# Sliding-window attention and maxout feed-forward on one core: Q and K of two batches loaded in groups of six tiles and transposed on the tensor engine, in a new order

## The chip, the cores and the metric

The kernel runs on one core of one Trainium2 chip. The metric is device time in microseconds (us), and lower is better. Executions of one kernel differ by a few tenths of a microsecond, so each comparison below takes several executions of both kernels on the same chip.

Engines: PE is the tensor engine, PEld its weight loads, DVE the vector engine, ACT the scalar engine, POOL is GpSimd, SP is the engine whose queue issues nearly all transfers. PE writes its results into PSUM, in units called banks; an eviction copies one from there to SBUF and frees the bank. The pitch of a kind of work is the time from one start to the next. "Landing" is the moment at which all data of a transfer have arrived.

## The reference

```python
# B, H, S, D = 4, 8, 768, 64;  n_global = 8;  n_local = 96
scores = q @ k.T / sqrt(D)                       # per batch and head
keep   = (key < n_global) | (0 <= query - key < n_local)
scores = scores + bias(head, distance)           # linear in the distance, one slope a head
a      = softmax(where(keep, scores, -1e9))
x      = (a @ v) laid out as 3072 tokens x 512
h      = maximum(maximum(x @ w1, x @ w2), x @ w3)   # d_ff = 768
return h @ w_out                                 # float32, 3072 x 512
```

## The kernel before

The 3072 tokens are 24 tiles of 128, six to a batch. A query tile needs only its own keys, those of the tile before and the eight global keys (copied into the tile before). Everything is cast to bf16. Q and K need their head dimension on the partitions, so they must be transposed; so must the attention result x before the feed-forward matmuls. Each transposition can be done in two ways: on PE (a matmul with the identity into a PSUM bank, then an eviction by ACT or DVE) or by a DMA transpose on the SP queue, which costs PE nothing.

What each engine does, and when, is a string of units. Each engine works through its own share of the string in order:

- `lG.p`, `cG.p`, `xG.p`: load, cast and transpose on PE part p of group G of tiles (Q and K);
- `LT`, `CT.0`, `XT`: load, cast and transpose Q and K of a single tile T (`XT.4` is a DMA transpose);
- `v`, `S`, `M`, `A`: load of v, scores with exp, mask multiply on DVE, attention output of a tile; a score unit whose last digit is 1 adds the bias on PE instead of having a mask multiplied later; `G` and `V` copy the global keys and values;
- `TT`: transpose x of tile T (`.4` by DMA, else on PE);
- `Fc.f.j`: first feed-forward matmuls of chunk c; `O` and `E`: second feed-forward and store; `w`, `W`, `o`, `Q`: load and cast weights; `K`, `B`: masks and biases; `D`: warm-up matmuls.

A group of sz tiles is loaded with sz consecutive tokens to a partition, so one row of a transfer is sz x 256 bytes: 512, 1024 or 1536.

```python
GROUPS = [[0, 2], [2, 2], [4, 2], [6, 4], [10, 2]]   # first tile, tiles
sizes = [4, 2, 2, 4, 4, 4, 4]                        # tiles of a feed-forward chunk
...
xb_pool  = ctx.enter_context(tc.tile_pool(name="xb", bufs=3))
ost_pool = ctx.enter_context(tc.tile_pool(name="ost", bufs=4))
psH = ... bufs=3   # tag "h":  feed-forward, and half of the transposes
psT = ... bufs=1   # tag "tp": transposes

def load_part(n, s):
    ...
    nc.sync.dma_start(out=r, in_=src.rearrange("h (i e) d -> i h (e d)", e=sz))

def u_x(n, s, how):                  # a part of a group, transposed on PE
    ...
    for e in range(sz):
        for j in range(lo, hi):
            nc.tensor.transpose(tp[:, e, j - lo], ..., identb)
    ...
    copy(dst[:, lo:hi], tp.rearrange("c e j i -> c j i e"))   # dst "c j (i e) -> c j i e"

def u_XT(T, how):                    # x of tile T
    ...
    if how == 4:
        nc.sync.dma_start_transpose(out=xT[c][:, :, i * 128:(i + 1) * 128], in_=...)
        return
    ...                              # else four PE transposes and one copy

def f2_out(po, c, tt, copy, ...):    # final eviction and store
    ost = ost_pool.tile(...)
    copy(ost, po)
    dma.dma_start(out=out[...], in_=ost)
```

The softmax here doesn't subtract the row's maximum and nothing guards it: scores larger than these inputs give would overflow.

Of the kernel before, what the change touches and what calls it, by code (L numbers as in the profile page):

```python
# [22 lines left out]


SCHEDULE = """
    K0 K1 K2 K3 K4 K5 l1.0 l1.1 D0.3 c0.0.2 B0.1 B1.1 B2.1 B3.0 K6 B4.1 B5.1 c0.1.1 c1.0.2 x0.0.4 B6.1
    B7.1 x0.1.4 S0.0.1 v0 l2.0 l2.1 K7 S0.1.1 G0.0 S1.0.1 S1.1.0 x1.0.3 c1.1.2 M0.0 M0.1 M1.0 v1 x1.1.4
    C0.1.2 v2 A0.1 G1.2 S2.0.1 M1.1 c2.0.2 x2.0.1 C1.1.1 S2.1.0 G2.2 S3.0.1 M2.0 M2.1 C2.1.1 T0.1 S3.1.1
    M3.0 M3.1 c2.1.2 v3 A1.0 C3.1.0 w0.0 V1.2 x2.1.2 w1.0 A2.1 V2.2 A3.0 T1.0 T2.1 T3.1 W1.0.1 W0.0.0
    G3.2 S4.0.0 S4.1.0 F0.0.0 F0.1.0 M4.0 F0.2.0 F0.3.0 G4.1 S5.0.0 M4.1 S5.1.0 w0.1 W0.1.1 w0.2 W0.2.2  # L30
    V3.2 F0.0.1 F0.1.1 F0.0.2 F0.1.2 v4 C4.1.0 A4.0 V4.2 w1.1 W1.1.2 W2.0.0 F0.4.0 F0.5.0 M5.0 M5.1 w1.2
    W1.2.2 v5 W2.1.0 T4.0 F0.2.1 F0.3.1 l3.0 l3.2 F0.4.1 l3.1 c3.0.2 c3.2.2 F0.5.1 o2 C5.1.0 A5.1 l3.3
    F0.2.2 Q2.2 F0.3.2 W2.2.0 o0 T5.0 F0.4.2 o1 F0.5.2 x3.0.0 F1.0.0 F1.1.0 c3.1.1 F1.2.0 x3.2.0 Q0.2
    F1.0.1 F1.1.1 F1.2.1 l4.0 l4.1 c3.3.0 F1.0.2 F1.1.2 F1.2.2 x3.1.2 x3.3.1 F1.3.0 F1.4.0 Q1.2 F1.3.1
    S6.0.0 S6.1.0 v6 v7 v8 G6.0 F1.3.2 F1.5.0 v9 c4.0.1 F1.4.1 S7.0.0 S7.1.0 G7.2 v10 M6.0 M6.1 M7.0
    M7.1 O0.0.0 F1.4.2 c4.1.1 C6.1.2 C7.1.2 L12 F1.5.1 S8.0.0 S8.1.0 x4.0.0 O0.1.0 A6.0 x4.1.2 A7.1 V7.2
    F1.5.2 v11 T6.0 O0.2.0 T7.1 G8.2 C8.1.2 S9.0.0 S9.1.0 G9.1 v12 v13 O0.3.0 F2.0.0 F2.1.0 S10.0.0 M8.0
    M8.1 M9.0 M9.1 S10.1.0 C9.1.2 L13 L14 F2.0.1 F2.1.1 F2.0.2 A8.0 C12.0.1 F2.1.2 G10.2 O1.0.0 V8.2
    A9.1 X12.1 M10.0 M10.1 C10.1.0 C11.1.0 F2.2.0 S11.0.0 S11.1.0 M11.0 M11.1 L15 F2.3.0 F2.4.0 O1.1.0
    V9.2 A10.1 F2.2.1 V10.2 T8.0 F2.3.1 F2.5.0 T9.0 A11.1 F2.4.1 T10.0 F2.2.2 F2.3.2 T11.1 F2.4.2  # L40
    S12.0.0 S12.1.0 F2.5.1 C13.0.2 C14.0.2 C15.0.1 X13.4 F3.0.0 F3.1.0 F3.0.1 G12.1 C12.1.0 F3.2.0
    F3.1.1 F3.2.1 S13.0.0 S13.1.0 F2.5.2 v14 C13.1.0 C14.1.2 M12.0 M12.1 F3.0.2 F3.1.2 X14.4 F3.2.2
    X15.4 G13.2 M13.0 M13.1 S14.0.0 S14.1.0 F3.3.0 F3.4.0 F3.5.0 M14.0 M14.1 G14.1 A12.0 A13.1 F3.3.1
    F3.4.1 F3.5.1 S15.0.0 M15.0 S15.1.0 G15.0 v15 V13.2 L16 L17 v16 T12.4 v17 M15.1 O2.0.0 C15.1.0 A14.0
    V14.2 F3.3.2 F3.4.2 T13.4 F3.5.2 C16.1.0 C16.0.2 X16.3 T14.4 C17.0.2 A15.1 X17.4 O2.1.0 S16.0.0
    S16.1.0 G16.1 L18 V15.2 L19 T15.1 M16.0 O3.0.0 M16.1 F4.0.0 F4.1.0 F4.0.1 F4.1.1 C18.0.2 L20 C19.0.2
    A16.1 F4.2.0 F4.3.0 S17.0.0 S17.1.0 F4.2.1 F4.0.2 F4.3.1 v18 M17.0 v19 M17.1 X18.3 X19.4 C20.0.0
    V16.2 F4.1.2 C17.1.2 O3.1.1 A17.1 F4.2.2 F4.3.2 S18.0.0 M18.0 S18.1.0 M18.1 F4.4.0 T16.4 T17.4
    F4.4.1 C18.1.2 C19.1.1 F4.4.2 X20.4 G18.1 S19.0.0 S19.1.0 F4.5.0 L21 M19.0 M19.1 v20 F4.5.1 A18.0
    T18.4 F4.5.2 A19.1 T19.4 V19.1 C21.0.1 X21.4 G19.1 L22 C22.0.2 L23 X22.4 O3.2.1 O3.3.0 O4.0.1  # L50
    S20.0.0 S20.1.0 M20.0 G20.0 O4.1.0 F5.0.0 F5.1.0 F5.2.0 S21.0.0 S21.1.0 G21.2 F5.0.1 F5.1.1 M20.1
    M21.0 F5.3.0 F5.0.2 F5.1.2 F5.2.1 F5.2.2 v21 C20.1.1 C21.1.2 F5.4.0 S22.0.0 M21.1 S22.1.0 C23.0.0
    F5.3.1 M22.0 M22.1 F5.5.0 F5.3.2 A20.0 V20.2 G22.2 v22 F5.4.1 X23.4 v23 F5.5.1 T20.4 A21.1 V21.1
    T21.4 F5.4.2 F5.5.2 S23.0.0 S23.1.0 M23.0 O4.2.0 M23.1 C22.1.2 A22.0 C23.1.0 O4.3.0 V22.2 T22.4
    A23.1 T23.4 O5.0.1 O5.1.0 O5.2.1 O5.3.0 F6.0.0 F6.1.0 F6.0.1 F6.0.2 F6.2.0 F6.3.0 F6.4.0 F6.1.1
    F6.2.1 F6.1.2 F6.3.1 F6.4.1 F6.2.2 F6.3.2 F6.5.0 F6.4.2 F6.5.1 F6.5.2 E
"""


# [450 lines left out]
```

## Time and profile before

The median was 180.36 us, from 180.34 to 180.45 in three runs. From the page of the profile (span 178.5 us):

| | busy us | share of the span |
|---|---|---|
| PE | 167.1 | 94% |
| DVE | 119.1 | 67% |
| ACT | 103.2 | 58% |
| POOL | 37.4 | 21% |
| main DMA queue (time of its packets over 16 engines) | | 83.6% |
| DMA packets, of them under 512 bytes | 83,587 / 66,160 | |

Read it so: one engine stands out, and it is PE. But a share of the whole span is an average over stages. The stretches that the prediction shows give the stages: until 23.3 us PE has gaps, from there to 172 us it has almost none, and then come the final stores.

I use three measures of a trace throughout: the start (until the first feed-forward matmul begins), the body (from there until the first of the final evictions begins) and the tail (from the first to the last of those evictions). Before, they end at 23.27, 172.04 and 175.46 us: the body takes 148.77 us and the tail 3.42.

### The profile page before, as it was taken

The numbers are of one execution on the slowest core, as the hardware profiler recorded it, in microseconds if no ns is written. First come the engines' busy times: TensorE is split into PE (matmuls) and PEld (weight loads), VectorE is DVE, ScalarE is ACT, GpSimd is POOL, SyncE is SP. The second block draws the span as 40 slices with busy tenths as digits, with TensorE's granted clock in tenths as the row PEclk, the third lists the DMA queues.
The fourth block names the chain that finished last, engine by engine and source line by source line (L and its number), as shares of the span: only waits on it lengthen the run. The fifth ranks groups of instructions, "written<-read, shape, count | busy, mean of one in ns | idle before, by whom it ended". The sixth has DMA issues, their size and how long they took to land.

```text
span 178.5 us, 3963 instructions
## 1 busy us (share of the span) xinstructions
PE 167.1 (94%) x1529; PEld 95.9 (54%) x1551; DVE 119.1 (67%) x237; ACT 103.2 (58%) x160; POOL 37.4 (21%) x65
## 2 busy tenths in 40 slices
...
GB/s 139 292 270 243 357 321 383 319 361 356 252 194 229 218 254 227 142 204 234 92 90 122 167 253 231 145 172 152 182 156 300 123 129 147 252 12 4 0 47 190
DMA packets 83587, 35.52 MB, mean 199 GB/s; under 512 B 66160, under 2 KB 78320, under 8 KB 83568
## 3 DMA queue, kind: packets, MB, share of 16 engines
q1 hardware_dynamic: 83424, 35.20, 83.6%
...
q10 hardware_dynamic: 144, 0.07, 0.1%
...
HBM read 25.17 MB, written 6.29 MB: 176 GB/s over the span
## 4 chain that ended last, share of the span: by engine, by line
PE 88%; ACT 3%; DVE 2%; POOL 2%; issue 1%; DMA 1%; POOLq 0%; ACTq 0%
PE h L361 53%; PE po L376 16%; PE sp L283 7%; PE op L322 3%; PE op L325 3%; PE tpp L239 3%; PE xtp L349 2%; ACT wmask L300 2%; PE sp L275 2%; DMA out_dram<-ost 1%; DVE qkT L243 1%; DVE xb L332 1%; ACT ost L382 1%; ACT P L288 1%; PE tp L261 1%
## 5 line engine op out<-in xcount | busy, mean ns | idle before, releaser
L361 PE MATMUL h<-xT,w 128*128 128x512 bf16 (+1 forms) x491 | 99.2, 348 | 0.7 <-issue 0.2
L361 PEld LDWEIGHTS <-w 128*128 128x128 bf16 x504 | 47.0, 98 | 40.4 <-ACT w L427 0.2
L288 ACT ACTIVATE P<-sp 128x1024 bf16<-128x1024 f32 (+1 forms) x48 | 43.4, 954 | 20.4 <-PE sp L283 20.2
L368 DVE TENSOR_TENSOR h<-h,h 128x512 bf16<-128x512 bf16 (+1 forms) x42 | 25.2, 609 | 25.6 <-PE h L361 15.5
L366 ACT CAST h<-h 128x512 bf16<-128x512 f32 (+1 forms) x42 | 21.6, 532 | 21.5 <-PE h L361 21.3
L376 PE MATMUL po<-wo,ht 128*128 128x512 bf16 (+2 forms) x147 | 33.1, 362 | 0.5
L370 DVE TENSOR_TENSOR ht<-h,h 128x512 bf16<-128x512 bf16 (+1 forms) x42 | 25.0, 606 | 3.7 <-PE h L361 3.0
L307 DVE TENSOR_TENSOR P<-P,wmask 128x1024 bf16<-128x1024 bf16 x36 | 24.8, 716 | 3.6 <-ACT P L288 3.5
L382 ACT COPY ost<-po 128x512 f32<-128x512 f32 (+2 forms) x20 | 11.2, 564 | 18.4 <-PE po L376 11.2
L376 PEld LDWEIGHTS <-ht 128*128 128x128 bf16 x156 | 14.0, 98 | 13.8
L332 DVE TENSOR_TENSOR xb<-op,rz 128x512 bf16<-128x512 f32 x24 | 16.6, 691 | 0.8
L283 PEld LDWEIGHTS <-qkT 64*128 64x128 bf16 x352 | 10.2, 96 | 10.0 <-issue 8.0
L283 PE MATMUL sp<-qkT 64*128 64x128 bf16 x352 | 15.2, 223 | 0.4 <-DVE xb L332 0.4
L322 PEld LDWEIGHTS <-P 128*128 128x128 bf16 x192 | 12.5, 97 | 2.7 <-ACT P L288 0.2
L221 POOL COPY va<-vaf 8x260 int32<-8x260 int32 x14 | 6.3, 449 | 34.7 <-PE op L325 34.7
L198 POOL CAST qkb<-raw 128x1024 bf16<-128x1024 f32 x7 | 7.2, 1037 | 27.6 <-DMA raw<-in_k_dram 27.6
L322 PE MATMUL op<-va,P 128*128 128x65 bf16 x160 | 12.4, 193 | 0.3 <-ACT va L189 0.2
L239 PE MATMUL tpp<-identb,qkp 128*128 128x128 bf16 x96 | 8.5, 246 | 4.0 <-POOL qkp L183 3.5
L325 PEld LDWEIGHTS <-P 128*128 128x128 bf16 x160 | 10.4, 97 | 1.8 <-issue 0.2
L239 PEld LDWEIGHTS <-qkp 128*128 128x128 bf16 x96 | 7.0, 112 | 5.8 <-POOL qkp L183 4.4
L325 PE MATMUL op<-va,P 128*128 128x65 bf16 x128 | 9.9, 193 | 0.1
L243 ACT COPY qkT<-tpp 128x1024 bf16<-128x1024 bf16 (+1 forms) x9 | 7.9, 873 | 3.4 <-PE tpp L239 3.4
...
## 6 DMA issues: line engine op xcount, KB each, us to landing
...
rawp<-in_q_dram SPq DMA_DIRECT2D x6, 512.0 KB, 7.3
rawp<-in_k_dram SPq DMA_DIRECT2D x6, 512.0 KB, 7.7
...
wst<-in_moe_w_dram SPq DMA_DIRECT2D x3, 512.0 KB, 8.6
```

The source lines that it names most:

```text
L239: nc.tensor.transpose(tp[:, e, j - lo], qb["p", n, s][:, e, 2 * j:2 * j + 2].rearrange("i h d -> i (h d)"), identb)
L283: nc.tensor.matmul(sp[:, hh, j2, ds], qT(T - ds, 1)[hsl, jp], qT(T, 0)[hsl, jp], start=not how, stop=True, skip_group_check=True)
L288: nc.scalar.activation(P[:, :, 0:n], sp.rearrange("p a b d n -> p (a b) d n")[:, :, 0:n], AF.Exp, bias=0.0, scale=scale)
L307: nc.vector.tensor_mul(P, P, wmask[:, g, :, 0:2])
L322: nc.tensor.matmul(o, P[:, i, 0], heads(va[T])[:, h], start=True, stop=(t == 0), skip_group_check=True)
L325: nc.tensor.matmul(o, P[:, i, 1], heads(va[T - 1])[:, h], start=False, stop=True, skip_group_check=True)
L332: nc.vector.tensor_tensor(out=x.rearrange("p (g h) d -> p g h d", g=2), in0=o4[:, :, :, 0:64], in1=rz[:, :, :, None].to_broadcast([128, 2, ...
L361: nc.tensor.matmul(ps, w123[f // 2][:, dm, j, (f % 2) * 128:(f % 2) * 128 + 128], xT[c][:, dm], start=(dm == 0), stop=(dm == 3))
L366: nc.scalar.copy(h01, ps)
L368: nc.vector.tensor_max(h01s[c, f], h01s[c, f], ps)
L370: nc.vector.tensor_max(ht[c][:, f], h01s[c, f], ps)
L376: nc.tensor.matmul(po, ht[c][:, f, tt * 128:(tt + 1) * 128], wo[:, f, cols], start=(f == 0), stop=(f == NF - 1))
```

## The change

The intent: Q and K of two whole batches (tiles 6 to 17) come in two groups of six tiles with rows of 1536 bytes and are transposed on PE. Before, it was one group of four and one of two in batch 1, and single tiles with rows of 256 bytes after that. This should relieve the DMA queue, which then has room for more transposes of x by DMA. The whole order was planned anew.

```diff
-    GROUPS = [[0, 2], [2, 2], [4, 2], [6, 4], [10, 2]]
+    GROUPS = [[0, 2], [2, 2], [4, 2], [6, 6], [12, 6]]

 SCHEDULE = """
-    K0 K1 K2 K3 K4 K5 l1.0 l1.1 D0.3 c0.0.2 B0.1 B1.1 B2.1 B3.0 K6 B4.1 B5.1 c0.1.1 c1.0.2 x0.0.4 B6.1
-    ... (all 31 lines of the order)
+    K0 K1 l1.0 l1.1 B0.1 B1.1 B2.2 B3.1 B4.0 B5.0 B6.1 c0.0.0 B7.1 c0.1.1 c1.0.2 x0.0.3 K2 K3 K4 x0.1.4
+    ... (all 32 lines of the order)
```

Counted from the two orders:

| | before | after |
|---|---|---|
| Q and K transposes on PE (128x128) | 120 | 144 |
| Q and K tiles transposed by DMA | 9 | 6 |
| x tiles transposed on PE / by DMA | 13 / 11 | 8 / 16 |
| score units with the bias on PE | 6 | 7 |
| warm-up units | 1 | 0 |
| tiles of Q and K loaded one by one | 12 | 6 |

More of the change, by code (lines that the diff above doesn't have):

```diff
@@ L25 @@
 SCHEDULE = """
-    K0 K1 K2 K3 K4 K5 l1.0 l1.1 D0.3 c0.0.2 B0.1 B1.1 B2.1 B3.0 K6 B4.1 B5.1 c0.1.1 c1.0.2 x0.0.4 B6.1
-    B7.1 x0.1.4 S0.0.1 v0 l2.0 l2.1 K7 S0.1.1 G0.0 S1.0.1 S1.1.0 x1.0.3 c1.1.2 M0.0 M0.1 M1.0 v1 x1.1.4
-    C0.1.2 v2 A0.1 G1.2 S2.0.1 M1.1 c2.0.2 x2.0.1 C1.1.1 S2.1.0 G2.2 S3.0.1 M2.0 M2.1 C2.1.1 T0.1 S3.1.1
-    M3.0 M3.1 c2.1.2 v3 A1.0 C3.1.0 w0.0 V1.2 x2.1.2 w1.0 A2.1 V2.2 A3.0 T1.0 T2.1 T3.1 W1.0.1 W0.0.0
-    G3.2 S4.0.0 S4.1.0 F0.0.0 F0.1.0 M4.0 F0.2.0 F0.3.0 G4.1 S5.0.0 M4.1 S5.1.0 w0.1 W0.1.1 w0.2 W0.2.2
@@ L31 @@
-    V3.2 F0.0.1 F0.1.1 F0.0.2 F0.1.2 v4 C4.1.0 A4.0 V4.2 w1.1 W1.1.2 W2.0.0 F0.4.0 F0.5.0 M5.0 M5.1 w1.2
-    W1.2.2 v5 W2.1.0 T4.0 F0.2.1 F0.3.1 l3.0 l3.2 F0.4.1 l3.1 c3.0.2 c3.2.2 F0.5.1 o2 C5.1.0 A5.1 l3.3
-    F0.2.2 Q2.2 F0.3.2 W2.2.0 o0 T5.0 F0.4.2 o1 F0.5.2 x3.0.0 F1.0.0 F1.1.0 c3.1.1 F1.2.0 x3.2.0 Q0.2
-    F1.0.1 F1.1.1 F1.2.1 l4.0 l4.1 c3.3.0 F1.0.2 F1.1.2 F1.2.2 x3.1.2 x3.3.1 F1.3.0 F1.4.0 Q1.2 F1.3.1
-    S6.0.0 S6.1.0 v6 v7 v8 G6.0 F1.3.2 F1.5.0 v9 c4.0.1 F1.4.1 S7.0.0 S7.1.0 G7.2 v10 M6.0 M6.1 M7.0
@@ L36 @@
-    M7.1 O0.0.0 F1.4.2 c4.1.1 C6.1.2 C7.1.2 L12 F1.5.1 S8.0.0 S8.1.0 x4.0.0 O0.1.0 A6.0 x4.1.2 A7.1 V7.2
-    F1.5.2 v11 T6.0 O0.2.0 T7.1 G8.2 C8.1.2 S9.0.0 S9.1.0 G9.1 v12 v13 O0.3.0 F2.0.0 F2.1.0 S10.0.0 M8.0
-    M8.1 M9.0 M9.1 S10.1.0 C9.1.2 L13 L14 F2.0.1 F2.1.1 F2.0.2 A8.0 C12.0.1 F2.1.2 G10.2 O1.0.0 V8.2
-    A9.1 X12.1 M10.0 M10.1 C10.1.0 C11.1.0 F2.2.0 S11.0.0 S11.1.0 M11.0 M11.1 L15 F2.3.0 F2.4.0 O1.1.0
-    V9.2 A10.1 F2.2.1 V10.2 T8.0 F2.3.1 F2.5.0 T9.0 A11.1 F2.4.1 T10.0 F2.2.2 F2.3.2 T11.1 F2.4.2
@@ L41 @@
-    S12.0.0 S12.1.0 F2.5.1 C13.0.2 C14.0.2 C15.0.1 X13.4 F3.0.0 F3.1.0 F3.0.1 G12.1 C12.1.0 F3.2.0
-    F3.1.1 F3.2.1 S13.0.0 S13.1.0 F2.5.2 v14 C13.1.0 C14.1.2 M12.0 M12.1 F3.0.2 F3.1.2 X14.4 F3.2.2
-    X15.4 G13.2 M13.0 M13.1 S14.0.0 S14.1.0 F3.3.0 F3.4.0 F3.5.0 M14.0 M14.1 G14.1 A12.0 A13.1 F3.3.1
-    F3.4.1 F3.5.1 S15.0.0 M15.0 S15.1.0 G15.0 v15 V13.2 L16 L17 v16 T12.4 v17 M15.1 O2.0.0 C15.1.0 A14.0
-    V14.2 F3.3.2 F3.4.2 T13.4 F3.5.2 C16.1.0 C16.0.2 X16.3 T14.4 C17.0.2 A15.1 X17.4 O2.1.0 S16.0.0
@@ L46 @@
-    S16.1.0 G16.1 L18 V15.2 L19 T15.1 M16.0 O3.0.0 M16.1 F4.0.0 F4.1.0 F4.0.1 F4.1.1 C18.0.2 L20 C19.0.2
-    A16.1 F4.2.0 F4.3.0 S17.0.0 S17.1.0 F4.2.1 F4.0.2 F4.3.1 v18 M17.0 v19 M17.1 X18.3 X19.4 C20.0.0
-    V16.2 F4.1.2 C17.1.2 O3.1.1 A17.1 F4.2.2 F4.3.2 S18.0.0 M18.0 S18.1.0 M18.1 F4.4.0 T16.4 T17.4
-    F4.4.1 C18.1.2 C19.1.1 F4.4.2 X20.4 G18.1 S19.0.0 S19.1.0 F4.5.0 L21 M19.0 M19.1 v20 F4.5.1 A18.0
-    T18.4 F4.5.2 A19.1 T19.4 V19.1 C21.0.1 X21.4 G19.1 L22 C22.0.2 L23 X22.4 O3.2.1 O3.3.0 O4.0.1
@@ L51 @@
-    S20.0.0 S20.1.0 M20.0 G20.0 O4.1.0 F5.0.0 F5.1.0 F5.2.0 S21.0.0 S21.1.0 G21.2 F5.0.1 F5.1.1 M20.1
-    M21.0 F5.3.0 F5.0.2 F5.1.2 F5.2.1 F5.2.2 v21 C20.1.1 C21.1.2 F5.4.0 S22.0.0 M21.1 S22.1.0 C23.0.0
-    F5.3.1 M22.0 M22.1 F5.5.0 F5.3.2 A20.0 V20.2 G22.2 v22 F5.4.1 X23.4 v23 F5.5.1 T20.4 A21.1 V21.1
-    T21.4 F5.4.2 F5.5.2 S23.0.0 S23.1.0 M23.0 O4.2.0 M23.1 C22.1.2 A22.0 C23.1.0 O4.3.0 V22.2 T22.4
-    A23.1 T23.4 O5.0.1 O5.1.0 O5.2.1 O5.3.0 F6.0.0 F6.1.0 F6.0.1 F6.0.2 F6.2.0 F6.3.0 F6.4.0 F6.1.1
@@ L56 @@
-    F6.2.1 F6.1.2 F6.3.1 F6.4.1 F6.2.2 F6.3.2 F6.5.0 F6.4.2 F6.5.1 F6.5.2 E
+    K0 K1 l1.0 l1.1 B0.1 B1.1 B2.2 B3.1 B4.0 B5.0 B6.1 c0.0.0 B7.1 c0.1.1 c1.0.2 x0.0.3 K2 K3 K4 x0.1.4
+    S0.0.1 S0.1.1 G0.0 x1.0.3 c1.1.2 K5 K6 S1.0.1 S1.1.1 v0 v1 x1.1.2 K7 C0.1.1 G1.2 C1.1.1 M0.0 M0.1
+    A0.0 M1.0 M1.1 A1.1 S2.0.1 T0.1 v2 C2.1.1 S2.1.1 G2.2 V1.1 l2.0 v3 M2.0 C3.1.2 T1.1 c2.0.1 l2.1
+    S3.0.0 S3.1.1 G3.0 M2.1 M3.0 A2.0 V2.2 c2.1.2 w0.0 W0.0.2 x2.0.2 M3.1 A3.1 w0.1 T2.0 x2.1.4 T3.0
+    S4.0.0 S4.1.0 M4.0 G4.0 W0.1.2 w0.2 F0.0.0 F0.1.0 w1.0 W1.0.2 W0.2.0 W2.0.0 V3.1 v4 F0.0.1 S5.0.0
@@ new lines @@
+    S5.1.0 F0.1.1 F0.0.2 F0.1.2 F0.2.0 F0.3.0 M4.1 M5.0 w1.1 M5.1 C4.1.2 A4.1 F0.4.0 F0.5.0 W2.1.1 V4.1
+    W1.1.2 T4.0 F0.2.1 w1.2 W1.2.0 F0.3.1 F0.4.1 l3.0 W2.2.1 v5 l3.4 l3.1 l3.5 C5.1.2 l3.2 F0.5.1 c3.0.0
+    c3.4.2 F0.2.2 x3.0.2 l3.6 A5.0 l3.3 F0.3.2 F0.4.2 l3.7 o1 o2 x3.4.2 c3.1.2 o0 T5.1 c3.5.0 F0.5.2 v6
+    c3.2.2 c3.6.2 F1.0.0 x3.1.3 v7 x3.5.0 l4.0 c3.3.2 v8 v9 F1.0.1 F1.1.0 F1.1.1 Q1.2 x3.2.1 F1.2.0
+    F1.3.0 x3.6.2 c3.7.1 l4.4 F1.2.1 x3.3.3 x3.7.0 F1.0.2 F1.1.2 S6.0.0 M6.0 S6.1.0 F1.3.1 F1.4.0 G6.0
@@ new lines @@
+    S7.0.0 S7.1.0 Q2.1 F1.2.2 l4.1 l4.5 F1.4.1 F1.3.2 C6.1.1 F1.4.2 G7.2 S8.0.0 S8.1.0 Q0.2 G8.2 O0.0.0
+    C7.1.1 O0.1.0 F1.5.0 c4.0.0 c4.4.2 l4.2 l4.6 v10 M6.1 M7.0 M7.1 M8.0 M8.1 A6.0 A7.1 V7.2 l4.3 l4.7
+    C8.1.0 O0.2.0 x4.0.3 F1.5.1 S9.0.0 v11 C9.1.2 S9.1.0 T6.1 O0.3.0 F1.5.2 G9.2 S10.0.0 S10.1.0 T7.1
+    c4.1.2 c4.5.2 x4.4.2 O1.0.0 M9.0 M9.1 M10.0 A8.0 F2.0.0 F2.1.0 T8.4 V8.2 x4.1.2 x4.5.0 F2.0.1 c4.2.2
+    c4.6.2 A9.0 F2.2.0 F2.0.2 M10.1 G10.0 F2.1.1 S11.0.0 T9.4 S11.1.0 C10.1.2 F2.2.1 M11.0 V9.2 O1.1.0
@@ new lines @@
+    x4.2.2 c4.3.1 c4.7.2 M11.1 A10.0 F2.3.0 F2.4.0 C11.1.1 x4.6.2 x4.3.2 F2.1.2 V10.2 A11.1 T10.4 T11.4
+    x4.7.0 F2.2.2 F2.3.1 S12.0.0 S12.1.0 M12.0 F2.3.2 F2.5.0 G12.1 S13.0.0 S13.1.0 G13.2 F2.4.1 L18
+    F2.5.1 F2.4.2 F2.5.2 S14.0.0 S14.1.0 F3.0.0 M12.1 v12 v13 M13.0 M13.1 C18.0.2 F3.0.1 v14 F3.1.0
+    F3.2.0 v15 v16 F3.3.0 M14.0 C12.1.1 A12.1 C13.1.0 G14.1 C14.1.2 M14.1 O2.0.0 A13.1 F3.1.1 V13.2 L19
+    T12.4 F3.0.2 A14.0 F3.2.1 F3.1.2 T13.4 S15.0.0 S15.1.0 G15.2 v17 V14.2 M15.0 F3.3.1 C15.1.0 C16.1.1
```

12 lines of the change are left out of this document (added).

## The prediction

> **What bounds the kernel now.** I read the page's busy table first (TensorE, PE, is busy 94% of 178.5 us), then the windows of the whole span cut where the work changes character, then the chain of waits in order of time, then the groups of instructions with shapes kept apart, then the landing times of single transfers. In the windows the columns are the stretch, its length, then busy us (instructions) of PE, PEld, DVE, ACT, POOL, then granted clock, DMA share, GB/s.
>
> ```profile
> 0.00:6.20 6.20, 1.48 (x4) 0.30 (x5) 2.81 (x18) 3.93 (x8) 3.23 (x13) 1.00 0.71 182
> 6.20:13.20 7.00, 6.53 (x56) 4.10 (x57) 2.52 (x5) 4.95 (x11) 2.85 (x4) 1.00 1.23 278
> 13.20:23.30 10.10, 8.77 (x152) 6.07 (x150) 9.32 (x18) 8.26 (x11) 3.18 (x6) 1.00 1.18 305
> 23.30:48.00 24.70, 24.54 (x208) 15.17 (x210) 18.45 (x31) 17.31 (x26) 9.01 (x10) 1.00 1.11 336
> 48.00:100.00 52.00, 51.53 (x578) 33.22 (x587) 40.09 (x85) 36.17 (x59) 11.60 (x20) 1.00 0.90 179
> 100.00:172.00 72.00, 71.42 (x519) 35.21 (x527) 45.63 (x81) 30.26 (x45) 7.53 (x12) 1.00 0.68 149
> 172.00:178.50 6.50, 2.79 (x25) 1.83 (x23) 0.29 (x1) 2.30 (x5) 0.00 (x0) 0.91 0.45 161
> ```
>
> Three stages. From 23.3 us (first feed-forward matmul) to 172 us PE is busy 147.5 of 148.7 us: nothing but the sum of its own work counts there. DMA is saturated to about 48 us, yet PE never waits for it after 23.3. Before 23.3 PE waits for first data and for short round trips over ACT and DVE. The last 6.5 us are the final eviction and store.
>
> A busy PE is not one at its peak, so I checked the stream by the chain of waits (start, length, engine, tile, line, count), which gives the pitch of each kind of work:
>
> ```profile
> 7.69 1.01 PE tpp L239 x8
> ...
> 17.57 0.51 PE sp L275 x2
> ...
> 33.20 0.22 PE xtp L349 x4
> 33.42 3.45 PE h L361 x16
> ...
> 41.04 0.45 PE tpp L239 x8
> 41.48 1.31 PE h L361 x12
> ...
> 52.64 0.55 PE sp L283 x16
> ```
>
> So warm pitches are 0.056 us a transpose (0.45/8), 0.216 us a 512-column feed-forward matmul (3.45/16), 0.109 us at 256 columns (1.31/12), 0.034 us a score matmul; 16 attention-output matmuls take 0.48 us in the same chain. Work from 23.3 to 172.04: 360 x 0.216 + 144 x 0.109 feed-forward, 131 x 0.215 output, 292 x 0.034 scores, 296 x 0.030 attention output, 72 x 0.056 Q/K transposes, 36 x 0.055 of x: about 146.6 us in 148.7. At most 2 us of slack lie in the body. What can change is the start (13.8 us of 23.3 are not warm work), the sum of PE work, and any new stall.
>
> **What the Trainium skill says.** (1) "TensorE: Matmul & The Clock Gate", Part 1, gives about 107 ns between 128-column matmuls while the array is cold and 56 ns warm, after about 3.4 us of sustained work. The trace agrees: 1.01 us for eight transposes at 7.69 (126 ns), 0.45 us at 41.04; the last cold eight end at 13.23 (0.98 us in the chain). The granted-clock column stays 1.00, so it does not show this gate. (2) Its Part 4 speaks of some 275 ns for a transpose in one kernel; here a record lasts 219 ns but eight start within 0.45 us, so I count the pitch. (3) "VectorE: DVE Perf Modes", What auto-detection actually checks: packed modes want 16-bit operands at step 1. The evictions of grouped transposes write interleaved tokens, and the trace agrees for DVE, whose copy of the same shape takes 678 ns contiguous (L266) and 1222 ns interleaved; ACT does not care (0.86 ns an element):
>
> ```profile
> L243 ACT COPY qkT<-tpp 128x1024 bf16<-128x1024 bf16 x6 | 6.1, 1020 | 2.7 <-PE tpp L239 2.7
> L243 DVE COPY qkT<-tpp 128x1024 bf16<-128x1024 bf16 x3 | 3.7, 1222 | 4.3 <-PE tpp L239 4.3
> L243 DVE COPY qkT<-tpp 128x512 bf16<-128x512 bf16 x3 | 2.1, 685 | 0.0
> L243 ACT COPY qkT<-tpp 128x512 bf16<-128x512 bf16 x3 | 1.7, 580 | 0.7 <-PE tpp L239 0.7
> L266 DVE COPY qkT<-tp 128x1024 bf16<-128x1024 bf16 x1 | 0.7, 678 | 0.0
> ```
>
> (4) "DMA: Bandwidth & Descriptors", Why small descriptors are slow, charges each packet a fixed cost. The trace's packet records agree: 21.7 ns for 256 bytes, 33.2 for 512, 52.6 for 1024, 93.5 for 2048.
>
> **The change, part by part, counted from the two orders.**
>
> PE work. Q and K of tiles 0 to 17 now go through PE, not tiles 0 to 11 and three more: 144 transposes for 120, +24 x 0.056 = +1.33 us. Attention results go through PE for 8 tiles rather than 13 (16 by DMA transpose rather than 11): 20 fewer transposes, -1.10 us. Score units that add the bias on PE instead of multiplying by a mask on DVE: 7 for 6, and one S0 pair stays small, so two more 512-column matmuls, +0.43 us, before the body. The three warm-up matmuls go; they ran at 1.19 to 2.65 us while PE had no data. Body +0.2 us, whole +0.7 us.
>
> DMA. The 256-byte Q/K loads of 6 tiles go: 12,288 packets x 21.7 ns = -267 us of engine time. Batch 1 loses 2048 x 52.6 and 2048 x 33.2, -176 us. The two groups of six add 4096 packets of 1536 bytes, estimated 73 ns by interpolation, +299 us. With 3 fewer large and 5 more small DMA transposes about -155 us over 16 engines, or 10 us of DMA time. It lies beside a PE that waited for no DMA in the body: worth nothing directly.
>
> Evictions and casts. Sixteen group evictions of 768 interleaved elements: estimated 0.80 us on ACT (580 + 256 x 0.86 ns) for 12 of them, 0.95 us on DVE (685 + 256 x 1.05) for 4. Against them go the old group and single-tile copies, five ACT casts of v, and most T copies: my tally is ACT -2 us, DVE +1 us (4 extra us of v casts and evictions against Q/K casts, one mask less), POOL about even. All three stay well under PE.
>
> The start. Loads land in queue order at a steady rate. The first weights landed 6.2 us after issue at 15.08, 21.3 us, behind ten earlier loads:
>
> ```profile
> wst<-in_moe_w_dram SPq DMA_DIRECT2D x1, 512.0 KB, 6.2
> ```
>
> The new order has the same ten loads ahead of it, so the same landing, then a POOL cast (1.04 us): not before 22.4. I walked the new order with the trace's durations: first Q part cast on ACT after two masks and two biases to 6.5 (before: POOL to 6.1), scores of tile 0 at 9.2, x1 parts until 14.3, tile 2 from 15.6 (its scores need an ACT copy that ends at 15.9; before, 14.1), tile 3 to 19.4, outputs of tiles 2 and 3 at 19.6 and 20.5, T3 at 22.2, its copy at 23.2, first feed-forward at 23.4. The gain of fewer masks up front is eaten by S1 put ahead of x1. I take the start as 0 +- 0.8 us.
>
> The middle. The order wants scores of tile 6 about 24.0 us after the first feed-forward unit (the warm work listed between: 15.5 + 2.7 + 3.9 + 1.9), at 47.4. All 3 MB of batch 1 must have landed, been cast, transposed and evicted by then, where before 2 MB sufficed. From the landing times before (w1.2 at 34.2 us, then about 1.1 us for each 384 KB) the eighth part lands at 44.1, is cast by 44.7 and evicted by 46.2: 1.2 us in hand.
>
> Sum: 180.36 + 0.0 (start) + 0.43 (bias, partly in idle time: say 0.2) + 0.2 (body) + 0.2 to 0.4 for stalls at new evictions = 181.0.
>
> **Rivals.** (a) DMA relief pays: lighter packets let weights and batch 1 come sooner. For it: DMA share over 1.1 until 48 us. Against: after 23.3 PE waits for no load; the first loads keep their 512-byte rows. At best 1 us at the start: 179.4. (b) A new wait at tile 6: the parts are late, or the 768-element evictions, one transposed bank each, hold the banks shared with the feed-forward, of which there are three. With eight stalls of 0.3 us or a late part by 2 us: 183. For it, DVE already works 40 of 52 us from 48 to 100; against, ACT has slack and takes 12 of the 16. (c) More tiles by DMA transpose, with three xb buffers and one in-order SP queue, delay outputs in the second half: 11 such transposes cost PE nothing before, at 2.4 us each to land; were the last before the final chunk late, 1 to 2 us, 182. (d) The missing warm-up leaves PE cold one 3.4 us window longer: at most +1.7 us of PE work, half of it in idle time: 181.8. Against: the warm-up ended 3.5 us before the first transpose and PE was still cold after it.
>
> **Range and chances.** The body cannot shrink below its work, so a gain over 2% (below 176.8) would need 3.6 us from the start, where the weights land no earlier: 1%. A loss over 2% (above 184.0) needs two rivals together: 6%. Median 181.0, 8 in 10 between 179.7 and 182.9.
>
> **What would show it.** Right: the first feed-forward matmul at 22.6 to 24.2 us; PE busy about 99% from there to its last matmul; 144 Q/K transposes at 0.056 us in the chain; evictions of 0.8 and 0.95 us; fewer packets under 512 bytes; and no longer idle time before PE. Wrong: PE idle around 44 to 50 us released by DMA casts or evictions, PE waiting for xb by DMA transpose in the second half, cold pitch after 14 us, or the first feed-forward matmul well before 22.4.

## The result, and the profile after

The changed kernel took 180.56 us (median of four runs, 180.48 to 180.85). The kernel before took 180.35 in the same rounds (180.31 to 180.45). The ratio is 1.0013, with a 95% interval of 0.9998 to 1.0028: the same. A ratio is always the mean time of one kernel's fast runs over that of the other's in the same rounds, so it is not quite the ratio of the medians.

The page of the changed kernel's profile:

```profile
PE 165.4 (93%) x1534; PEld 95.2 (53%) x1554; DVE 121.3 (68%) x240; ACT 103.0 (58%) x160; POOL 38.4 (22%) x65
...
DMA packets 70820, 35.39 MB, mean 198 GB/s; under 512 B 53393, under 2 KB 65553, under 8 KB 70801
```

There are 12,767 packets fewer, and the span is 178.7 us for 178.5. The windows of the changed kernel, with the columns as in the prediction (stretch, length, then busy us and instructions of PE, PEld, DVE, ACT and POOL, granted clock, DMA share, GB/s):

```profile
6.20:13.20 7.00, 6.70 (x72) 4.25 (x72) 4.48 (x6) 5.68 (x12) 2.29 (x3) 1.00 1.28 256
13.20:23.30 10.10, 8.07 (x141) 5.37 (x138) 7.30 (x16) 8.89 (x13) 3.38 (x6) 1.00 1.16 312
23.30:48.00 24.70, 24.54 (x219) 15.27 (x221) 19.12 (x34) 17.23 (x27) 9.76 (x11) 1.00 1.06 341
48.00:100.00 52.00, 51.63 (x589) 33.35 (x594) 41.58 (x88) 38.63 (x59) 13.95 (x24) 1.00 0.97 209
100.00:172.00 72.00, 71.47 (x500) 35.00 (x509) 45.16 (x80) 26.36 (x42) 5.46 (x9) 1.00 0.58 125
```

From 23.3 to 172 us PE is busy 24.54 + 51.63 + 71.47 = 147.64 us; before it was 147.49. The stretch is full in both kernels, so its length is the sum of its work. The DMA share falls a little between 13 and 48 us and clearly from 100 us on (0.58 for 0.68), where PE waited for no transfer anyway. In the stretch of 48 to 100 us it even rises (0.97 for 0.90): most of the second group of six is loaded there.

The start, and two pitches, in the chain of waits of the changed kernel (start, length, engine, tile, line, count):

```profile
12.37 7.86 DMA rawp<-in_k_dram
...
20.27 1.05 POOL qkp L184
...
21.37 0.41 PE tpp L240 x4
21.80 0.59 ACT qkT L244
...
22.44 0.73 PE sp L284 x16
23.17 0.32 PE h L362
...
42.07 0.67 PE tpp L240 x12
```

Here the chain goes back to the K half of tiles 4 and 5, which takes 7.86 us from issue to landing, then a cast, four transposes, an eviction, and sixteen score matmuls of tile 4 that stand in PE's order just ahead of the feed-forward. The last line gives the warm pitch of the new transposes: 0.67/12 = 0.056 us. The sizes of the new evictions stand in the groups of instructions (line, engine, operation, shapes, count, then busy us and mean ns, then idle time before them):

```profile
L244 ACT COPY qkT<-tpp 128x768 bf16<-128x768 bf16 x12 | 9.4, 801 | 4.4 <-PE tpp L240 4.3
...
L244 DVE COPY qkT<-tpp 128x768 bf16<-128x768 bf16 x4 | 3.8, 954 | 0.4 <-PE tpp L240 0.3
```

Estimated were 0.80 and 0.95 us. The middle, where batch 1 must be ready for tile 6, stands in the timeline of the changed kernel:

```profile
45.36 0.55 DVE L184 CAST qkp<-rawp 128x768 bf16<-128x768 f32 x1
...
46.73 0.80 ACT L244 COPY qkT<-tpp 128x768 bf16<-128x768 bf16 x1 [0.31 <-PE tpp L240]
...
47.50 0.40 PE L284 MATMUL sp<-qkT 64*128 64x128 bf16 x8
```

The eighth part of the group is cast from 45.36 to 45.91, its eviction ends at 47.53, and the scores of tile 6 begin at 47.50 (the eviction's data are read only by the later four of these eight matmuls, and the first of those that waits for ACT begins at 47.63). PE loses at most 0.1 us here, and no more than 0.1 us is in hand.

| | first feed-forward | body | tail | median |
|---|---|---|---|---|
| before | 23.27 | 148.77 | 3.42 | 180.35 |
| after | 23.10 | 149.10 | 3.43 | 180.56 |
| difference | -0.17 | +0.33 | +0.01 | +0.21 |

The first three columns come from one trace each, and one trace is not exact to tenths. Five of the traces below share the old start order, and in them the first feed-forward matmul starts at 23.06 to 23.47 us; six share the new one, with 23.02 to 23.41. So -0.17 is not shown to be a gain. The ratio above does not separate the two kernels either.

The order, the loads and the choice of engines have all changed, and the time has not moved. The question is where the relief of the queue went, and whether any part of the change is worth something by itself. My theory: the body is bound by the sum of PE work, and that sum is nearly unchanged because two large terms cancel. The wide groups put 24 transposes more on PE, the DMA transposes of x take 20 off it, and the freed queue is what lets those be issued. The rivals: a good part and a bad part (a better start and a worse body, or the reverse) cancel; or the DMA transposes could have been had without the wide groups.

### The profile page after: what moved, and what is told of

It is laid out like the page before. It is cut to its first block, busy times and chain, and to the rows that moved or that the text cites. A ratio compares the mean times of both kernels' runs of the same rounds, so it can differ in the third digit from the quotient of the medians.

```text
span 178.7 us, 3987 instructions
## 1 busy us (share of the span) xinstructions
PE 165.4 (93%) x1534; PEld 95.2 (53%) x1554; DVE 121.3 (68%) x240; ACT 103.0 (58%) x160; POOL 38.4 (22%) x65
## 4 chain that ended last, share of the span: by engine, by line
PE 83%; SPq 6%; DMA 6%; issue 1%; ACT 1%; POOL 1%; ACTq 0%
PE h L362 53%; PE po L377 16%; PE sp L284 6%; DMA rawp<-in_k_dram 4%; SPq L175 3%; PE tpp L240 3%; SPq L159 3%; PE op L323 3%; PE op L326 2%; DMA out_dram<-ost 1%; PE xtp L350 1%; ACT ost L383 1%; POOL qkp L184 1%; ACT qkT L244 0%; ACTq L383 0%
## 5 line engine op out<-in xcount | busy, mean ns | idle before, releaser
L308 DVE TENSOR_TENSOR P<-P,wmask 128x1024 bf16<-128x1024 bf16 x35 | 24.0, 709 | 3.6 <-ACT P L289 3.6
L383 ACT COPY ost<-po 128x512 f32<-128x512 f32 (+2 forms) x19 | 10.6, 562 | 19.6 <-PE po L377 17.9
L240 PE MATMUL tpp<-identb,qkp 128*128 128x128 bf16 x144 | 12.0, 233 | 7.3 <-ACT qkp L184 6.5
L244 ACT COPY qkT<-tpp 128x768 bf16<-128x768 bf16 (+2 forms) x16 | 12.6, 801 | 5.4 <-PE tpp L240 5.3
L240 PEld LDWEIGHTS <-qkp 128*128 128x128 bf16 x144 | 9.9, 104 | 9.0 <-ACT qkp L184 6.5
L184 POOL CAST qkp<-rawp 128x768 bf16<-128x768 f32 (+1 forms) x14 | 12.2, 878 | 11.2 <-DMA rawp<-in_k_dram 6.0
L323 PEld LDWEIGHTS <-P 128*128 128x128 bf16 x192 | 12.5, 97 | 2.6 <-DVE rz L332 0.3
L199 POOL CAST qkb<-raw 128x1024 bf16<-128x1024 f32 x5 | 5.2, 1040 | 22.3 <-DMA raw<-in_k_dram 22.3
## 6 DMA issues: line engine op xcount, KB each, us to landing
wst<-in_moe_w_dram SPq DMA_DIRECT2D x3, 1024.0 KB, 10.7
```

The lines of the kernel that those rows point to most:

```text
L240: nc.tensor.transpose(tp[:, e, j - lo], qb["p", n, s][:, e, 2 * j:2 * j + 2].rearrange("i h d -> i (h d)"), identb)
L308: nc.vector.tensor_mul(P, P, wmask[:, g, :, 0:2])
L323: nc.tensor.matmul(o, P[:, i, 0], heads(va[T])[:, h], start=True, stop=(t == 0), skip_group_check=True)
```

## The experiments

Twelve kernels ran, in three sets of four. All outputs are right. The kernel before had medians of 180.35, 180.44 and 180.44 us in the three sets.

### Set 1: start, body, and the swaps one at a time

**h1_newstart.** The new order up to the first feed-forward unit, then the old order, with the old groups.

```diff
 SCHEDULE:
-  (before's units up to F0.0.0)
+  (after's units up to F0.0.0, without w0.1 W0.1.2 w0.2, which the rest of before's order has)
   (before's units from F0.0.0 on, without M4.0 and G4.1; w1.0 W1.0.1 come just ahead of them)
```

> The changed kernel's order up to its first feed-forward unit, then the old kernel's order for all that is left (old groups, no warm-up). Theory 'work': the time is the start plus the sum of the tensor engine's work. The new start reaches the first feed-forward matmul at 23.1 us (old 23.27), the old body takes 148.8 us: about 180.2 us, ratio to before 0.999. Rival 'carried over': the queue order of the new start makes later loads late and the old body waits: 180.5 us or more, with idle time before TensorE after 23 us.

Measured: 181.04 us (180.93 to 181.15), ratio 1.0039 (1.0027 to 1.0051). The first feed-forward matmul starts at 23.06, so the new start is reproduced to 0.04 us. But the body came out at 149.32, and my theory (180.2 us) missed: the rival's sign, over 180.5 us with idle time after 23 us, is what came. Part of the longer body is my splice. PE's timeline of this run:

```profile
25.32 1.90 PE L360 MATMUL h<-xT,w 128*128 128x512 bf16 x8 [0.37 <-DVE w L426]
```

PE waits 0.37 us for a weight cast that the splice put behind a mask multiply in DVE's order. The last stores also landed later than before, which I could not explain. What follows: no gain of the start alone is shown, and an order is not a list of independent pieces.

**h2_oldstart.** The converse: the old start, then the new order.

```diff
 SCHEDULE:
-  (after's units up to F0.0.0)
+  (before's units up to F0.0.0, without w1.0 W1.0.1, then w0.1 M4.0 G4.0 W0.1.2 w0.2)
   (after's units from F0.0.0 on, with the groups of six)
```

> The old order up to the first feed-forward unit, then the changed kernel's order. Theory 'work': first feed-forward matmul at about 23.3 us and a body of 149.1 us: 180.7 us, ratio 1.002. Rival 'DMA relief pays': the wide rows shorten the body, and only the new start costs: 180.2 us or less.

Measured: 180.68 us (180.62 to 181.57), ratio 1.0028 (1.0013 to 1.0043). The body is 149.01 us, within 0.1 of the changed kernel's. In these traces the new body is 0.2 to 0.3 us longer than the old one whichever start it has, and there is no large good part hidden behind a large bad one.

**l2_early.** In the chain the start hangs on the landing of tiles 4 and 5, so I moved their loads ahead of v of tiles 2 and 3.

```diff
-  v0 v1 ... v2 ... l2.0 v3 ... l2.1
+  v0 v1 l2.0 l2.1 ... v2 ... v3
```

> The changed kernel with the two loads of tiles 4 and 5 moved ahead of the third and fourth load of v. Theory: the chain of waits of the changed kernel is right that the landing of the second of them (20.2 us) sets its start; it would land by about 16.5 us, and the first feed-forward matmul moves from 23.1 to 22.8 us, where the cast of the first weights (landed 21.7) stops it: about 180.25 us. Rival: the ACT and DVE round trips of tiles 2 and 3 set the start: unchanged at 180.55 us.

Measured: 181.93 us (181.84 to 181.93), ratio 1.0087 (1.0074 to 1.01). My expectation fell. PE's timeline of this run:

```profile
21.01 0.19 PE L322 MATMUL op<-va,P 128*128 128x65 bf16 x1 [0.83 <-POOL va L189]
```

Now the attention output of tile 3 waits 0.83 us for v, and the first feed-forward matmul comes at 24.07 instead of 23.10. The queue is full in this stretch (DMA share 1.16 and 1.28 in the windows above), so each load arrives just in time, and moving one forward makes another late. The last landing in the chain was not the one surplus wait; it was the last of several that were all about equally late.

**dma_transposes.** The rival that the DMA transposes could be had alone: before's order and groups, with x of tiles 8 to 11 and Q and K of tiles 12 and 18 transposed by DMA where the order has them.

```diff
-  T8.0 ... T9.0 ... T10.0 ... T11.1      X12.1      X18.3
+  T8.4 ... T9.4 ... T10.4 ... T11.4      X12.4      X18.4
```

> The old kernel with six transposes (attention results of tiles 8 to 11, Q and K of tiles 12 and 18) given from TensorE to DMA: 32 transposes fewer on TensorE. Theory 'work': 32 x 0.056 = 1.8 us off the body: 178.6 us, ratio 0.990. Rival: the transposes' latency on the one in-order queue makes TensorE wait for them: 180 us or more, with idle time before the scores or the feed-forward.

Measured: 186.32 us (185.44 to 186.9), ratio 1.0313 (1.0291 to 1.0334). Nearly two microseconds of PE work less made the kernel six slower. The windows of this run around the place, with the columns as above:

```profile
73.00:78.70 5.70, 0.26 (x4) 0.08 (x1) 1.07 (x3) 0.00 (x0) 0.00 (x0) 0.80 1.24 137
78.70:83.00 4.30, 4.30 (x21) 2.01 (x21) 2.05 (x5) 1.13 (x3) 0.00 (x0) 0.50 0.52 101
```

The same stretch of the kernel before:

```profile
73.00:78.70 5.70, 5.65 (x44) 3.35 (x44) 3.61 (x9) 3.36 (x6) 0.62 (x1) 1.00 1.03 165
```

PE stands still for 5.44 us, from 73.26 to 78.70. The trace's record of the granted clock falls to 0.50 at 76.47 us and is back at 1.00 at 83.30, so PE runs 4.6 us at 0.50, which costs about 2.3 more. The sum is -1.8 + 5.4 + 2.3 = +5.9; measured were +6.0. The Trainium skill, "TensorE: Matmul & The Clock Gate", Why this matters for your kernels, asks for no idle gaps of PE over some 3 us between bursts, or the clock goes back to half. This trace agrees: 5.44 us idle, then 0.50. The reason for the stall stands in the timeline of the same run, on DVE and on SP's queue:

```profile
71.70 7.83 SPq L339 DMA_TRANSPOSE xT<-xb  x4
...
77.63 0.69 DVE L331 TENSOR_TENSOR xb<-op,rz 128x512 bf16<-128x512 f32 x1 [5.44 <-DMA xT<-xb]
```

The 7.83 us reach from the first to the last of four transposes. Three of them hold the in-order queue for 1.4, 1.2 and 1.9 us; then it waits 1.9 us for the x of tile 11, and the fourth takes 1.2. DVE cannot write that x, because all three xb buffers are taken: the transpose of tile 8, whose data were ready at 64.72 us, is issued at 71.70 behind stores, loads and the transpose of tile 12, and lands at 77.53. Chunk 3, which needs x of tiles 8 to 11, comes very soon after in the old order.

### Set 2: is it the place, the buffers, or the order?

**dmaT_early.** The same kernel, with each of the four transposes right behind its attention output.

```diff
-  A8.0 ... T8.4 ... A9.1 ... T9.4 ... (T8 to T11 together, late)
+  A8.0 T8.4 ... A9.1 T9.4 ... A10.1 T10.4 ... A11.1 T11.4
```

> The same six transposes on DMA as in dma_transposes, but each of the four of attention results now stands in the order directly after its tile's output, ahead of stores and loads. Theory: in dma_transposes they were queued behind stores that wait for evictions, and the three xb buffers were held until then (DVE sat idle 5.4 us on it); issued at once they cost nothing, and the 32 transposes saved on TensorE show: 178.6 us, ratio 0.990. Rival: DMA transposes on this path stall whatever their place: above 180.3 us.

Measured: 186.58 us (185.71 to 187.05), ratio 1.0331 (1.0306 to 1.0357): no gain, my expectation fell. In the order of SP's queue the transpose of tile 12 and two single-tile loads now stand between, and the last two transposes are issued only from 75.75 us on, 4.5 and 4.0 us after their data are ready. PE's timeline:

```profile
79.68 0.59 PE L360 MATMUL h<-xT,w 128*128 128x512 bf16 x1 [2.98 <-DMA xT<-xb]
```

Before this wait PE had stood still for 1.72 us, until 75.77. The granted clock of this run falls to 0.50 at 77.06 us, when the second wait was 0.36 us old, so here a single pause of 3 us was not needed for it.

**dmaT_xb6.** dma_transposes with six xb buffers instead of three.

```diff
-    xb_pool = ctx.enter_context(tc.tile_pool(name="xb", bufs=3))
+    xb_pool = ctx.enter_context(tc.tile_pool(name="xb", bufs=6))
```

> dma_transposes unchanged but for six xb buffers instead of three. If the buffers are what made DVE wait, its 5.4 us wait goes and the time falls from 186.3 to between 178.6 and 181 us (what is left is a late start of the third feed-forward chunk). If the latency of the transposes is the cause, it stays above 185 us.

Measured: 186.39 us (186.03 to 187.12), ratio 1.0332 (1.0309 to 1.0355). The wait for a buffer is gone, and the time has not moved: the wait has gone over to the one that uses the data.

```profile
78.97 0.58 PE L360 MATMUL h<-xT,w 128*128 128x512 bf16 x1 [4.32 <-DMA xT<-xb]
```

So neither an earlier place in the order nor more buffers is enough. What is left, as I read the traces, is that four transposes must pass a queue that carries loads, stores and other transposes as well, and land (2.4 to 5.8 us after issue in these three runs) shortly before chunk 3 needs all four; no run tests this by itself. What the changed order does differently can be read from its own trace: its four transposes are issued within 0.7 us of their data being ready, and the last lands at 76.88 us, 1.4 us before chunk 3. On SP's queue between 60 and 85 us the old order has ten loads of single Q or K halves (7.9 us of the queue) and three Q and K transposes (5.5 us); the new one has two such loads (1.1 us) and four transposes of x, in two pairs that begin at 64.45 and 71.38 us and take 3.6 and 4.3 us. And PE has 5.6 us of other work between the last attention output of tile 11 (72.65 us) and chunk 3 (78.25 us), where the old order lists about 2.5 us (five units at 256 columns and the small scores of tile 12: 5 x 0.44 + 0.27). These runs show that the swap fails in the old order as it stands. They do not show that no order with the old groups could take it.

**ost6.** The tail: the last evictions wait for the store that reads their buffer, in the kernel before and after alike. The chain of the kernel before:

```profile
173.14 2.22 DMA out_dram<-ost
...
175.46 0.27 ACT ost L382
```

The experiment is the changed kernel with six buffers for the final evictions.

```diff
-    ost_pool = ctx.enter_context(tc.tile_pool(name="ost", bufs=4))
+    ost_pool = ctx.enter_context(tc.tile_pool(name="ost", bufs=6))
```

> The changed kernel with six output buffers instead of four, nothing else. In the chain of waits its last eviction waits 2.2 us for the store of an earlier tile to free a buffer. Theory: the last eviction starts at the last matmul's end, some 0.6 us earlier: 180.0 us. Rival: other stores set the end: 180.5 us.

Measured: 180.25 us (179.97 to 180.31), ratio 0.9986 (0.9973 to 0.9998). This is between the theory (180.0) and the rival (180.5). The tail shrank as expected, from 3.43 to 2.79 us. But the body of the traced execution grew by 0.36. The timeline of this run, POOL and DVE:

```profile
44.92 1.04 POOL L431 CAST wo<-wost 128x1024 bf16<-128x1024 f32 x1 [1.39 <-DMA wost<-in_moe_w_out_dram]
...
45.27 1.10 DVE L184 CAST qkp<-rawp 128x768 bf16<-128x768 f32 x1
```

This is the cast of the eighth part once more. It took 0.55 us in the changed kernel, where POOL's cast began at 46.14 us, after it. Here POOL's cast of a weight (1.04 us) began first, and DVE's took 1.10. The Trainium skill, "SBUF — State Buffer", SBUF: two separate sides, says that DVE, in the modes that use both of its ports, shares a pair of ports with GpSimd, and that whichever begins first keeps it for its whole instruction. The trace agrees: this record is twice as long as in the changed kernel. The thirteen other casts of this shape on DVE, in the seven traces with the groups of six and wide rows, took 0.55 us, and none of them began inside a POOL instruction. PE then waited about 0.3 us at 46.4. This is where the missing reserve in the middle of the changed order shows.

The two buffers can hardly have caused this. The first of them is written at 53.7 us, and in the changed kernel, t_on_pe and t_late, whose orders are the same up to there, POOL's cast begins at 46.14, 46.17 and 47.41 us. Whether the two casts meet thus differs from trace to trace without a change of the order ahead of them. Of ost6's five executions the traced one was the slowest (180.31 us); two took 179.97 and 180.03, near the theory, but they were not traced.

**t_on_pe.** The other side of the swap: the changed kernel with all 16 DMA transposes of x back on PE.

```diff
-  T8.4 T9.4 T10.4 ... T23.4
+  T8.0 T9.1 T10.0 ... T23.1        (copies by ACT and DVE in turn)
```

> The changed kernel with all sixteen DMA transposes of attention results put back on TensorE, evicted by ACT and DVE in turn: 64 more transposes. Theory 'work': 64 x 0.056 = 3.6 us on top of 180.55: 184.1 us, ratio to before 1.021. Rival 'TensorE has slack in the body': less than half of it, below 182.3 us. Rival 'evictions': well above it, over 186 us, with TensorE waiting for banks.

Measured: 193.02 us (192.69 to 193.37), ratio 1.0698 (1.0683 to 1.0714), so +12.5 us. The work of 64 transposes is 64 x 0.056 = 3.6 us. My theory (184.1 us) missed. The time is over the rival's mark of 186 us, but the reason is not the rival's. The rest is gaps: the time between successive PE starts beyond their pitch, from 23 us on, adds up to about 9 us more than in the changed kernel (18.2 for 9.2, in both of which missing records count as gaps). In those over 0.15 us the trace names DVE's write of xb for 6.3 us and the eviction of a bank for 0.7. One of them in PE's timeline:

```profile
146.11 0.40 PE L349 MATMUL xtp<-identb,xb 128*128 128x128 bf16 x4 [1.48 <-DVE xb L332]
```

A PE transpose that stands right behind the attention output waits for DVE to divide by the sums. A DMA transpose in the same place makes only the queue wait.

**Which of these is the cost of the swap, and which of its place**, is what the third set asks.

### Set 3: the place, the rows, and a better kernel

**t_late.** As t_on_pe, with each transpose moved behind at least 1.7 us of other PE work.

```diff
-  A8.0 F2.0.0 F2.1.0 T8.0 ... A9.0 F2.2.0 F2.0.2 F2.1.1 S11.0.0 T9.1 ...
+  A8.0 F2.0.0 F2.1.0 ... F2.0.1 A9.0 F2.2.0 T8.0 F2.0.2 ... O1.1.0 T9.1 ...
```

> As t_on_pe, but each of the sixteen transposes stands at least 1.7 us of TensorE work after its tile's attention output instead of right behind it. Theory: of the 12.5 us that t_on_pe cost, 3.6 are work and the rest waits for xb, so here nearly the work alone is left: 184 to 185 us. Rival: the evictions or the single transpose bank are what costs: above 188 us.

Measured: 187.29 us (186.96 to 187.56), ratio 1.038 (1.0364 to 1.0396). It lies between the theories. The place was worth 5.7 us of the 12.5. Of the +6.7 that remain, 3.6 are the work and about 3.5 are gaps (12.7 us for 9.2), now of another kind:

```profile
76.85 0.38 PE L349 MATMUL xtp<-identb,xb 128*128 128x128 bf16 x4 [1.22 <-ACT xT L350]
```

There is one PSUM bank for these transposes, and where two or more come together each waits for the eviction of the one before. So the DMA transposes of x spare the changed kernel 3.6 us of PE work that no place in the order would take away.

**narrow_rows.** The wide rows alone: the groups of six loaded tile by tile with rows of 256 bytes, all else as in the changed kernel. Then token and tile change places in the transposed data.

```diff
+        if sz == 6:
+            nc.sync.dma_start(out=r.rearrange("i h (e d) -> i h e d", e=sz),
+                              in_=src.rearrange("h (e i) d -> i h e d", e=sz))
+            return
...
-        dst = ....rearrange("c j (i e) -> c j i e", e=sz)
+        dst = ....rearrange("c j (e i) -> c j i e" if sz == 6 else "c j (i e) -> c j i e", e=sz)
```

> The changed kernel, but the two groups of six load their tokens tile by tile, in rows of 256 bytes instead of 1536; order, casts, transposes and evictions stay. Theory: DMA is saturated to about 48 us, and at 21.7 ns a packet of 256 bytes a 384 KB part costs 2.1 us of 16 engines instead of about 1.1, so the eighth part of batch 1 lands 5 to 8 us late and the scores of tile 6 wait for it: 185 to 189 us. Rival: the wide rows buy nothing because the loads are hidden: below 181.5 us.

Measured: 219.39 us (219.23 to 219.49), ratio 1.2158. The experiment is spoiled, and the groups of instructions say why:

```profile
L249 ACT COPY qkT<-tpp 128x768 bf16<-128x768 bf16 x12 | 42.3, 3693 | 3.1 <-PE tpp L245 3.0
```

The eviction now writes with a step of 128 elements and takes 3.7 us on ACT and 3.6 on DVE, for 0.80 and 0.95. The rows cannot be told from the evictions in the total. One reading stands by itself, since the queue issued these loads without a pause: the parts of the first group landed about 1.7 us apart, for 1.05 in the changed kernel, and the eighth at 49.1 us, for 43.6. With narrow rows the group of six would have missed tile 6. What the wide rows are worth in time stays open.

**ost6_slack.** ost6, with the wait in the middle given reserve: the last transpose of the group one unit later, and the scores of tile 6 one unit later.

```diff
-  x3.3.3 x3.7.0 F1.0.2 F1.1.2 S6.0.0 M6.0 S6.1.0 F1.3.1 ...
+  x3.3.3 F1.0.2 x3.7.0 F1.1.2 F1.3.1 S6.0.0 M6.0 S6.1.0 ...
```

> ost6 with the last Q/K part's transposes and the scores of tile 6 each one feed-forward unit later. In ost6 TensorE waited about 0.3 us for that part's cast, which took 1.10 us beside a GpSimd cast instead of 0.55 us. Theory: with 0.4 us more room the wait goes: 179.9 to 180.0 us. Rival: something else holds the body: 180.25 us as ost6.

Measured: 180.60 us (180.51 to 180.65), ratio 1.001 (0.9997 to 1.0022). My expectation fell. The wait in question went, but two new gaps of 0.28 and 0.27 us appeared at 46.1 and 49.3 us. The releasers in the trace name both. At 46.44 us the feed-forward unit that I moved forward starts when ACT ends a group eviction (46.40) and so frees one of the three banks that both use. At 49.64 us the second half of the scores of tile 7 starts when ACT has read the scores of tile 6 (49.60), which I had moved closer to it. Both follow from the moves themselves, and show how little room this stretch has.

**best_before.** What the runs point to: the kernel before, with six buffers at the end and one Q/K tile more by DMA (tile 18, one of the swaps of dma_transposes).

```diff
-    ost_pool = ... bufs=4
+    ost_pool = ... bufs=6
-    X18.3
+    X18.4
```

> The old kernel with six output buffers instead of four and Q and K of tile 18 transposed by DMA instead of TensorE. Theory: 0.55 us off the end, as ost6 showed at its end, and 8 x 0.056 = 0.45 us off the body: 179.4 us, ratio 0.9945. Rival: the DMA transpose stalls the scores of tile 18, as those of tile 12 stalled: 180 us or more.

Measured: 179.64 us (179.32 to 180.2), ratio 0.9964 (0.995 to 0.9977). The end of its chain:

```profile
168.98 5.22 PE po L375 x36
...
174.27 0.27 ACT ost L381
```

The time lies between the theory (179.4) and the rival (180), nearer the theory. No store stands in the chain any more; the last eviction follows the last matmul. In the trace, of the fastest of six executions, the tail is 2.83 us (3.42 before), and the body 148.38 (148.77); only these readings tell the two edits apart. This is below both kernels, by 0.4% of the kernel before, so still the same within 2%.

## Why the prediction was right

**The bound.** Right. The body is the sum of PE work. I predicted +0.2 us of work and +0.2 to 0.4 of stalls; the body grew by 0.33. How that divides is open: cut at each kernel's own body, PE is busy 147.56 and 148.04 us, so all of it would be busy time, but records can be missing and tenths are not safe. h2_oldstart gave the same body with another start. Two readings in the prediction were off without harm. The terms of its sum add to 146.4 us, and 280 score matmuls lie in the body, not 292 (the sixteen of tile 4 come before it), so the slack was nearer 2.7 us than 2. And 126 ns a cold transpose is a piece of the chain divided by eight; their starts are 107 ns apart, up to 13.44 us.

**The start.** Right in size: 23.4 with 0.8 either way, and it was 23.10. The weights bound it less clearly than I said. Their cast ended at 22.82, and the chain goes through Q and K of tile 4, whose scores stand ahead of the feed-forward. l2_early showed that this landing is not *the* cause either: several transfers come due together. No run moved the weights alone. The two additional bias matmuls lay in this stretch and did not show.

**The DMA term.** Its direction was right and its size off. Packets of 1536 bytes took 74.7 ns (73 estimated), but the sum of packet times fell by 70 us, not 155. The term mis-sized was that the other packets would keep their durations: those of 256 bytes took 23.2 ns instead of 21.7, and 51,200 x 1.43 ns give 73 us back; some 2,200 packets of 4 bytes give 16 more. Why they took longer is open. It lay beside PE, as I had it, so it had no effect on the time. Rival (a) was worth 0.2 us at the start at best, and not even that is shown.

**The middle.** The landing was right (44.1 predicted, 43.6 measured). "Is cast by 44.7 and evicted by 46.2: 1.2 us in hand" was the step that failed. I had let the cast begin when the data landed. In DVE's order it stands behind an eviction and a maximum and begins at 45.36; its eviction ends at 47.53. There was 0.1 us in hand. By chance there was also nothing missing; in the traced execution of ost6 one cast on POOL began earlier, and it cost 0.3 us. Rival (b) thus sits on the edge, unseen in the time: its late part showed in ost6, and its held bank in ost6_slack (0.28 us).

**The evictions.** 0.80 and 0.95 us predicted, 0.801 and 0.954 measured. My words for them were the wrong way round, though: they do not write interleaved tokens. They read PSUM with a step and write consecutively. narrow_rows, which does write with a step, shows what that would have cost.

**Rival (c)**, the latency of the DMA transposes, did not occur in the changed kernel, and I gave it 1 to 2 us. In the old order it is worth 6 (three runs). The new order has over 5 us of other work where it would have struck.

**Rival (d)**, the missing warm-up, did not occur: the pitch was warm from 10.7 us, before that of the kernel before (13.5). How much of this is luck is open: the cold phase ended at 11.4 to 13.5 us in the six traces with the warm-up unit and at 10.6 to 12.6 in the eight without it.

**Where the relief went.** Between 60 and 85 us the queue has fewer loads than before, and it is spent on transposes of x. That took 20 transposes off PE (1.1 us) and paid for the 24 that the groups put on it (1.3 us). Shown: that the new body depends on these transposes being by DMA (t_on_pe, t_late), and that the old order does not bear them (dma_transposes, dmaT_early, dmaT_xb6). Only argued: that the wide rows are what makes room for them, from the two queues' records, since narrow_rows was spoiled.

**The sum.** I had +0.6 us and it was +0.2. The prediction counted 0.2 for the bias and up to 0.6 for work and stalls in the body; in the traces the start came out 0.17 lower and the body 0.33 higher. Both differences are as small as those between traces of one order, so the close hit of the total is in part luck.

## What to carry to other kernels

Where one engine is busy 99% of a stage, count its work and nothing else: relief on a queue it does not wait for is worth only what is bought with it. Swapping the engine of a unit pays only if the order is planned around its latency; swaps of this kind in a fixed order cost 6 us in one direction (four tiles of x and two of Q and K to DMA) and 12.5 in the other (sixteen tiles of x to PE), and stalls of 3.0 to 5.4 us were paid again in clock. When an order is planned to the last tenth, look for the waits that cost nothing to remove (here two more buffers at the end: 0.6 us of the tail), and look at more than one trace before a change of some tenths is explained, because two engines can meet in one trace and not in another of the same order (0.3 us in ost6).

## What the Trainium skill lacked or had wrong

- "TensorE: Matmul & The Clock Gate", Part 4, has transposes at some 275 ns and outside the fast clock. Here twelve start within 0.67 us (56 ns each, warm) and one record lasts about 220 ns.
- The same page, Part 1, describes the cold phase at the start, and the traces show it (starts of transposes 107 ns apart). What it does not say is that the granted clock in a profile's windows reads 1.00 in that phase, and yet drops to 0.50 after a stall of 5.44 us in the middle: the trace of the kernel before has no clock record until 13.49 us, and that of the changed kernel none until 10.65, which is where the pitch turns warm. The end of the cold phase moved between 10.6 and 13.5 us from trace to trace.
- "SBUF — State Buffer" speaks of a penalty for accesses that leave a line, without a size. Writing 768 elements with a step of 128 took 3.7 us on ACT and 3.6 on DVE, for 0.80 and 0.95 written consecutively.
- "DMA: Bandwidth & Descriptors" gave me no figure for how long one small transpose from SBUF to SBUF holds the in-order queue that issues it. Here it was 1.2 us for most, for a tile of x (128x512) and for one of Q and K (128x1024) alike, and up to 3.1; and it landed 2.4 to 5.8 us after its issue in the three runs that moved x of tiles 8 to 11. This decided three experiments.
- The same page charges each small packet a fixed cost, and does not say how far its whole time varies. Here packets of 256 bytes took 21.7 ns in one kernel and 23.2 in the other.
